# Attention half blocks: value products and normalizing before the next score products

## The chip, the cores and the metric

One Trainium2 chip; the kernel runs on one of its cores. The metric is the device time of the whole program in microseconds (us), the median of several runs.

## What is computed

The reference is windowed attention over four batches of 768 tokens with eight heads of 64, followed by a mixture of eight experts, of which each token takes two. Cut to what matters:

```python
scores = scale * np.matmul(q, k.transpose(0, 1, 3, 2))
keep = is_global | is_local          # 8 first keys, and 96 keys back from the query
scores = np.where(keep, scores + bias, -1e9)
a = np.exp(scores - np.max(scores, axis=-1, keepdims=True))
a = a / (np.sum(a, axis=-1, keepdims=True) + 1e-09)
x = np.matmul(a, v)                  # [4, 8, 768, 64] -> [3072, 512]
logits = x @ w_gate + np.log1p(np.exp(x @ w_noise)) * noise
# the two largest logits of a token choose its experts and weigh them
out[mask] += top2_w * (np.maximum(x[mask] @ w1[e], 0.0) @ w2[e])
```

## The kernel before

The tokens are taken in 24 blocks of 128 queries, six to a batch. A block's eight heads are taken in two halves of four heads, so attention is a loop over 48 **half blocks**, written `for n in range(0, NPAIR, 2)` with n = 0, 2, ... 94. The order of the instructions on each engine is the order in which the program emits them; nothing reorders them later. Attention lies in the first 150 us of the span, the experts behind it.

The work is software-pipelined. Half block n of the loop emits, in this order:

- **score(n + 2)**: VectorE adds the bias to the scores of the next half block and takes the maximum of each row (L862, four instructions on two PSUM banks, x = 0 and 1, with two query halves s each); ScalarE takes the exponentials (L865, four instructions). Behind each of the four a `tick` may emit one step of a routing program that is under way, mostly a small VectorE instruction.
- **trans(n), trans(n + 1)**: the **transposes** of the probabilities on TensorE (L878: six of 128x128, or four in the first block of a batch), each half into its own one of two PSUM banks, and ScalarE's two copies of them to SBUF (L880).
- **gate_t**, in every second half block: four **gate transposes** of a finished block (L380) and ScalarE's copy of them (L389, tile `pair`).
- **product(n + 4)**: the **score products** of queries by keys two half blocks ahead (L848, 16 records on 64x64 tiles of the array) into the two banks of the ring "sc", which score(n + 2) must have read.
- **norm(n - 4)**: VectorE's division by the row sums (L910, L912, L915), with three ticks.
- **attend(n - 2)**: the **value products** (L899). In the first block of a batch they are 16 records on tiles of 128 rows and 64 columns. In every other block they come in two parts of 16 records: the **short part** (64 or 40 rows by 64 columns) and the **tall part** (128 or 104 rows by 64 columns).
- **gate_s** with halves (L426, four short products on 128x64 tiles; seven half blocks) and **gate_l** (L410, the **gate products**, 16 records on 128x32 tiles that read the tile `pair`, and ScalarE's copy of them, L413; mostly every fourth half block). Steps of the routing that remain follow in `finish`.

In the last half block, n = 94, attend stands before norm. With 48 half blocks, 45 (n = 2 to 90) have both value products and score products; in eight of these the value products are of a batch's first block.

Of the kernel before, what the change touches and what calls it, by code (L numbers as in the profile page):

```python
# [35 lines left out]
def tile_local_global_attention_then_moe(  # L36
# [45 lines left out]
    def bank(tag):  # L82
        ring = rings[tag]
        key = tuple(ring)
        turns[key] = turns.get(key, -1) + 1
        return psum.tile([P, 512], F32, name=tag, tag=f"b{ring[turns[key] % len(ring)]}", bufs=1)
# [139 lines left out]
    def words(x):  # L226
        return x.bitcast(U16).rearrange("p (d h) -> p h d", h=2)

    def planes(x):
        return x.rearrange("p (h d) -> p h d", h=2)  # L230

    def halved(to, frm):

        for c in range(KC):
            c = slice(c * P, (c + 1) * P)
            nc.gpsimd.tensor_copy(to[:, :, c], frm[:, :, c])  # L236
# [131 lines left out]
    def partner(g):  # L368
        if not windowed or g in ALONE:
            return None  # L370
        a = [a for a, z in SEG if a <= g < z][0]
        return (g - a) % 2

    def gate_t(g):
        x = rowed[g] = XR.pop(g).rearrange("p h d -> p (h d)")
        stored[g] = gp.tile([P, 2 * Dm], U16, name="xt", bufs=4)
        halved(planes(stored[g]), words(x))
        ps = bank("m").rearrange("p (k t) -> p k t", k=KC)
        for k in range(KC):
            nc.tensor.transpose(ps[:, k], x[:, k * P:(k + 1) * P], ident)  # L380
        j = partner(g)
        if j is None:
            XT[g] = ys[2].rearrange("p (k t) -> p k t", k=KC)
            to = XT[g]
        else:
            if j == 0:
                XT[g + 1] = pairs[0].rearrange("p (k j t) -> p k j t", k=KC, j=2)
            to = XT[g + 1 - j][:, :, j]
        nc.scalar.activation(to, ps, AF.Copy)  # L389
# [263 lines left out]
    with ExitStack() as actx:  # L653
# [127 lines left out]
        def empty_rows():  # L781
            nc.gpsimd.memset(zero, 0.0)
            o = xd[:DUMP].rearrange("(p r) d -> p r d", p=P)
            nc.sync.dma_start(o, zero.bitcast(U16)[:, None, :].to_broadcast(o.shape))
# [30 lines left out]
        def tick(place):  # L815
            for y in sorted(active, key=lambda y: y[1] != CLOSE):
                if y[0].ready <= place:
                    return go(y)
# [8 lines left out]
        def geo(n):  # L827

            g, u = divmod(n, HP)
            b, i = divmod(g, NB)  # L830
            return g, u, b, i
# [52 lines left out]
        def attend(n):  # L884

            g, u, b, i = geo(n)
            ps = pav[g, u // 2] = bank("av")[:, :4 * D1].rearrange("p (h d) -> p h d", h=4)
            at = [AT.pop(n + x) for x in range(2)]
            heads = [(at[x], 2 * y + x, y * Q) for x in range(2) for y in range(2)]
            parts = [[(vs[g], 0, P, 0)], [(vs[g], 0, P, 1)]]  # L890
            if i:
                parts = [[(vs[g], 0, Q, 2), (vp[g], 0, NP + NG, 0)], [(vp[g], Q, NP + NG, 2), (vs[g], 0, P, 1)]]
            n = len(parts[0])
            for k in range(n):
                for a, h, q0 in heads:
                    c = slice((u // 2 * 4 + h) * D1, (u // 2 * 4 + h + 1) * D1)
                    for s in range(2):
                        t, r, z, part = parts[s][k]
                        nc.tensor.matmul(ps[s * Q:(s + 1) * Q, h], a[r:z, part * P + q0:part * P + q0 + Q], t[r:z, c],  # L899
                                         start=k == 0 and (n == 1 or h == 0), stop=k + 1 == n,  # L900
                                         tile_position=(r, s * Q), skip_group_check=True)

        def norm(n):

            g, u, b, i = geo(n)
            ps = pav.pop((g, u // 2))
            if u == 0:
                XR[g] = ys[g % 2].rearrange("p (h d) -> p h d", h=H)
            den = aw.tile([P, 4], F32, name="den", bufs=2)
            nc.vector.tensor_scalar(den, ps[:, :, D], 1e-9, None, op0=OP.add)  # L910
            tick(4)
            nc.vector.reciprocal(den, den)  # L912
            tick(5)
            h0 = 2 * u
            nc.vector.tensor_mul(XR[g][:, h0:h0 + 4], ps[:, :, :D],  # L915
                                 den[:, :, None].to_broadcast([P, 4, D]))
            tick(6)
# [3 lines left out]
        def at(n, f, *a):  # L921
            todo.setdefault(n, []).append((f, a))

        NPAIR = NT * HP
# [65 lines left out]
        if not windowed:  # L990
            gate_consts()
            route_consts()
            empty_rows()
            empty_first()
            for j in range(NZ):
                zero_out(j)
            for g in range(NT):
                whole(g)
            load_w(NU)
            for j in range(FC):  # L1000
                split(0, 1, j)
            load_w(NU)
            for t in range(TA):
                turn(0, t)
        else:
            for k in range(HP):
                at(k, biases, bias, dist, (2 * k, 2 * k + 1))
            at(4, gate_consts)
            at(10, route_consts)
            at(66, empty_rows)  # L1010
            at(80, empty_first)
            for g in range(NT):
                b, i = divmod(g, NB)
                n = g * HP
                if g + 3 < NT:
                    at(n + 2, load_v, g + 3)
                if i % NBH == 0 and g + NBH < NT:
                    for k in range(NBH):
                        at(n + 4 * k, load_qk, *divmod(g // NBH + 1, 2), k)
            for j in range(NZ):  # L1020
                at(70 + 4 * j, zero_out, j)
            for j, (n, x, y) in enumerate(((8, 16, 18), (14, 22, 24), (28, 40, 50), (36, 52, 64))):
                at(n, load_w)
                at(x, split, 0, 1, j, nc.gpsimd)
                at(y, split, 0, 1, j + NU, nc.gpsimd)
            ends = [z - 1 for a, z in SEG]

            product(0)  # L1030
            product(2, "av")
            score(0)
            for n in range(0, NPAIR, 2):
                g, odd = divmod(n // 2 - LAG, 2)
                begin()
                if n + 2 < NPAIR:
                    score(n + 2)
                trans(n)
                trans(n + 1)
                if g >= 0:  # L1040
                    if odd:
                        if g in ends:
                            gate_s(g)
                            active.append((Steps(route(ends.index(g))), ends.index(g)))
                    else:
                        gate_t(g)
                if n + 4 < NPAIR:
                    product(n + 4)
                if n == NPAIR - 2:
                    attend(n - 2)  # L1050
                if n >= 4:
                    norm(n - 4)
                if 2 <= n < NPAIR - 2:
                    attend(n - 2)
                if g >= 0 and odd and g not in ends:
                    gate_s(g, True)
                if g >= 0 and not odd:
                    gate_l(g, (lambda *x: at(n + 4, *x)) if n + 4 < NPAIR else None)
                if n < NPAIR - 2:
                    finish()  # L1060
                for x in n, n + 1:
                    for f, a in todo.pop(x, []):
                        f(*a)
            for x, _ in [y for y in active if y[1] <= CLOSE]:
                for _ in x:
                    pass
            active[:] = [y for y in active if y[1] > CLOSE]
            begin()
            norm(NPAIR - 4)
            for t in range(TA):  # L1070
                turn(0, t, bank("sc" if t > 1 else "at"))
                if t == 1:
                    gate_t(NT - 2)
            attend(NPAIR - 2)
            gate_l(NT - 2)
            begin()
            norm(NPAIR - 2)
            finish()
            finish()
            routes[NT - 1] = route(len(SEG) - 1)  # L1080
            assert len(routes) == 1 and not todo
            pending = [x for x, _ in active] + [Steps(x) for x in routes.values()]
# [447 lines left out]
    with tc.If(left > 0), tc.tile_pool(name="lc", bufs=1) as lc:  # L1530
# [18 lines left out]
        for e in range(E):  # L1549
            n = nc.values_load(more[0:1, e:e + 1], min_val=0, max_val=N)  # L1550
# [72 lines left out]
```

## Time and profile before

| | us |
|---|---|
| median of 3 runs | 698.28 (698.16 to 698.64) |
| the profiled execution | 696.72 |
| its span, first to last instruction | 695.0 |
| TensorE busy in the span | 682.1 (98%) |
| VectorE / ScalarE / GpSimd busy | 460.0 / 423.7 / 323.8 |
| mean granted TensorE clock | 0.996 of full speed |

PE is TensorE's matmul, PEld its weight load, DVE VectorE, ACT ScalarE, POOL GpSimd. L848 is line 848 of the kernel. Matmuls are pipelined, so the start of the next phase, and not the end of a record, tells how long a phase held TensorE.

### The profile page before, as it was taken

What the parts mean: (1) busy time and instruction counts of PE and PEld (TensorE: products, weight loads), DVE (VectorE), ACT (ScalarE), POOL (GpSimd) and SP (SyncE); (2) the same over time, 40 slices, a digit from 0 to 9 for tenths busy, and PEclk for the clock granted to TensorE, in tenths of its full rate; (3) what the DMA queues carried; (4) which work ended last, traced back from release to release, by engine and by line L of the source; (5) the groups of instructions that cost most, each with busy time, mean ns of one, the idle gap of its engine ahead of it and who ended that gap; (6) DMA issues with size and microseconds to landing.
All of it is one profiled execution on the core that took longest, in us unless ns stands there. A gap on an engine that the chain in (4) does not pass through costs nothing. (4 is left out here: it accounts for less than half of the span.)

```text
span 695.0 us, 16022 instructions
## 1 busy us (share of the span) xinstructions
PE 682.1 (98%) x5701; PEld 615.7 (89%) x5701; DVE 460.0 (66%) x1412; ACT 423.7 (61%) x912; POOL 323.8 (47%) x408
## 2 busy tenths in 40 slices
PE   7999999999999999999999999999999999999995
PEld 5888888888889999999999998999998899889984
DVE  6668788968938578557846693777367757847600
ACT  6888787762346576557754764586458557745510
POOL 3352737350188672264536445552745344541222
PEclk9999999999999999999999999999999999999998
DMA  9999988859393986347845974596559557843233
GB/s 255 320 293 314 277 250 271 304 182 331 130 292 72 178 186 151 63 111 182 174 76 114 166 170 79 151 172 117 93 154 245 88 106 181 171 74 91 32 47 49
DMA packets 132889, 116.61 MB, mean 168 GB/s; under 512 B 51866, under 2 KB 97050, under 8 KB 132800
## 3 DMA queue, kind: packets, MB, share of 16 engines
q1 hardware_dynamic: 121392, 89.35, 46.8%
q0 software_dynamic: 11264, 25.89, 20.9%
q8 instruction: 47, 0.77, 0.5%
q14 instruction: 42, 0.34, 0.2%
q10 hardware_dynamic: 144, 0.26, 0.2%
HBM read 71.07 MB, written 33.10 MB: 150 GB/s over the span
## 5 line engine op out<-in xcount | busy, mean ns | idle before, releaser
L1426 PE MATMUL bank<-xh,wall 128*128 128x384 f32 (+4 forms) x784 | 216.0, 342 | 0.0
L1426 PEld LDWEIGHTS bank<-xh,wall 128*128 128x128 f32 x784 | 144.1, 188 | 3.2
L1426 PE MATMUL bank<-xl,wall 128*128 128x384 f32 (+4 forms) x392 | 133.4, 340 | 0.0
L1145 POOL DMA_INDIRECT out_dram<-y,ids x40 | 65.1, 1626 | 123.1 <-ACT y L1142 120.2
L1169 PE MATMUL av<-w2h,hh 128*128 128x512 f32 x304 | 119.6, 393 | 0.0
L1169 PE MATMUL av<-w2h,hl 128*128 128x512 f32 x304 | 119.1, 392 | 0.0
L1169 PE MATMUL av<-w2l,hh 128*128 128x512 f32 x304 | 119.0, 392 | 0.0
L197 DVE TENSOR_TENSOR wall<-raw,wall 128x512 fp32r<-128x512 f32 (+1 forms) x84 | 75.9, 910 | 52.4 <-ACT wall L196 51.9
L196 ACT ACTIVATE wall<-raw 128x512 fp32r<-128x512 f32 (+1 forms) x84 | 57.9, 699 | 45.7 <-POOL raw L1279 45.7
L1117 DVE SCALAR_TENSOR_TENSOR hl<-bank,hh 128x384 fp32r<-128x384 f32 (+4 forms) x84 | 47.1, 561 | 51.0 <-ACT hh L1113 50.5
L865 ACT ACTIVATE a<-ns,mx 128x168 f32<-128x168 f32 (+1 forms) x192 | 67.8, 421 | 14.5 <-DVE mx L862 14.1
L1426 PEld LDWEIGHTS bank<-xl,wall 128*128 128x128 f32 x392 | 73.9, 188 | 2.9
L251 POOL DMA_INDIRECT xg<-xd,ids x49 | 52.9, 1079 | 41.7 <-DVE place L302 29.8
L1169 PEld LDWEIGHTS av<-w2h,hl 128*128 128x128 f32 x304 | 57.1, 188 | 12.6
L862 DVE CUSTOM_DVE_ANT_0 ns<-sc,bias 128x168 f32<-128x168 f32 (+1 forms) x188 | 51.8, 320 | 24.6 <-PE sc L848 10.0
L1169 PEld LDWEIGHTS av<-w2l,hh 128*128 128x128 f32 x304 | 57.1, 188 | 9.3 <-DVE w2l L197 0.3
L1169 PEld LDWEIGHTS av<-w2h,hh 128*128 128x128 f32 x304 | 57.1, 188 | 9.2
L1113 ACT ACTIVATE hh<-bank 128x384 fp32r<-128x384 f32 (+4 forms) x84 | 41.8, 498 | 37.1 <-DVE bank L1500 24.2
L1278 POOL TENSOR_TENSOR raw<-raw 128x256 f32<-128x256 f32 x28 | 22.4, 802 | 83.0 <-DVE wall L197 82.4
L899 PE MATMUL av<-vs,at 128*64 128x65 f32 (+1 forms) x768 | 57.1, 224 | 0.2 <-issue 0.2
L236 POOL COPY xt<-y 128x256 uint16<-128x256 uint16 x96 | 35.0, 401 | 46.8 <-DVE y L915 45.4
L899 PEld LDWEIGHTS av<-vs,at 128*64 128x64 f32 (+1 forms) x768 | 50.8, 136 | 2.8 <-issue 1.9
(219 smaller groups left out, 1463.4 us busy)
## 6 DMA issues: line engine op xcount, KB each, us to landing
raw<-in_w SPq DMA_DIRECT2D x64, 256.0 KB
raw<-in_w SPq DMA_DIRECT2D x32, 512.0 KB
out_dram<-zero SPq DMA_DIRECT2D x14, 512.0 KB
vs<-in_v SPq DMA_DIRECT2D x24, 260.0 KB
xd<-xt SPq DMA_DIRECT2D x24, 256.0 KB
qbuf<-in_q SPq DMA_DIRECT2D x23, 256.0 KB
ks<-in_k SPq DMA_DIRECT2D x20, 272.0 KB
xe<-y SPq DMA_DIRECT2D x17, 256.0 KB
```

The costliest lines, as they stand in the source:

```text
L196: nc.scalar.activation(hi, src, AF.Copy)
L197: eng.tensor_sub(lo, src, hi.bitcast(F32))
L236: nc.gpsimd.tensor_copy(to[:, :, c], frm[:, :, c])
L251: nc.gpsimd.indirect_dma_start(out=xg[e, t].bitcast(U16)[:m], out_offset=None, in_=xd[:n], in_offset=bass.IndirectOffsetOnAxis(ap=r, axis= ...
L862: nc.vector.tensor_tensor_reduce(out=ns[x][:, s, :w], in0=ps[:, s], in1=bias[:, u + x, s] if i else bias0[:, u + x, s], scale=-scale, scal ...
L865: nc.scalar.activation(A[n + x][:, s * w:(s + 1) * w], ns[x][:, s, :w], AF.Exp, bias=mx[x][:, s:s + 1], scale=-1.0)
L899: nc.tensor.matmul(ps[s * Q:(s + 1) * Q, h], a[r:z, part * P + q0:part * P + q0 + Q], t[r:z, c], start=k == 0 and (n == 1 or h == 0), stop ...
L1113: nc.scalar.activation(inner(e)[0][j][:, f, :src.shape[1]], src, AF.Relu)
L1117: nc.vector.scalar_tensor_tensor(lo, src, 0.0, hi.bitcast(F32), op0=OP.max, op1=OP.subtract)
L1145: ins = nc.gpsimd.indirect_dma_start(out=out, out_offset=bass.IndirectOffsetOnAxis(ap=r, axis=0), in_=y, in_offset=None, bounds_check=N + ...
L1169: nc.tensor.matmul(ps, x[j][:, f, cols], w[:, f], start=n == 0, stop=n == 3 * FC - 1)
L1426: nc.tensor.matmul(ps, wb[c % 2][u][:, 2 * a + k], x[v][:, 2 * b + k], start=start and n == 0, stop=stop and n == 5, skip_group_check=True)
```

## The change

In every half block norm(n - 4) and attend(n - 2) are emitted before product(n + 4). The special place of attend in the last half block goes away: it now follows norm there as well. Nothing is added or left out.

```diff
+                if n >= 4:
+                    norm(n - 4)
+                if n >= 2:
+                    attend(n - 2)
                 if n + 4 < NPAIR:
                     product(n + 4)
-                if n == NPAIR - 2:
-                    attend(n - 2)
-                if n >= 4:
-                    norm(n - 4)
-                if 2 <= n < NPAIR - 2:
-                    attend(n - 2)
```

## Rows read from the trace of the kernel before

**Rows 1.** The page: busy time of each engine.

```profile
PE 682.1 (98%) x5701; PEld 615.7 (89%) x5701; DVE 460.0 (66%) x1412; ACT 423.7 (61%) x912; POOL 323.8 (47%) x408
```

**Rows 2.** Busy time by stretches behind attention: length, engines, PE clock, DMA.

```profile
160.00:200.00 40.00, 39.72 (x195) 32.11 (x195) 30.19 (x117) 12.28 (x25) 11.23 (x19) 1.00 0.76 267
200.00:600.00 400.00, 400.00 (x2229) 373.46 (x2228) 268.11 (x461) 250.23 (x472) 208.70 (x193) 1.00 0.68 142
```

**Rows 3.** TensorE in order of time (start, length, operation), an inner block.

```profile
104.43 0.87 PE L878 MATMUL at<-ident,a 128*128 128x128 f32 x6
105.23 0.80 PE L848 MATMUL sc<-ks,qbuf 64*64 64x168 f32 x16
105.86 0.22 PE L899 MATMUL av<-vs,at 64*64 64x65 f32 x1
...
106.44 0.27 PE L899 MATMUL av<-vs,at 128*64 128x65 f32 x1
...
106.90 0.22 PE L899 MATMUL av<-vs,at 128*64 128x65 f32 x1
107.05 0.87 PE L878 MATMUL at<-ident,a 128*128 128x128 f32 x6
107.76 0.60 PE L380 MATMUL m<-ident,y 128*128 128x128 f32 x4
108.29 0.67 PE L848 MATMUL sc<-ks,qbuf 64*64 64x128 f32 x16
```

**Rows 4.** The same view, value products of a batch's first block.

```profile
44.77 0.80 PE L848 MATMUL sc<-ks,qbuf 64*64 64x168 f32 x16
45.51 0.69 PE L899 MATMUL av<-vs,at 128*64 128x65 f32 x16
46.12 0.88 PE L878 MATMUL at<-ident,a 128*128 128x128 f32 x6
```

**Rows 5.** The same view, a half block without score products.

```profile
148.18 0.27 PE L899 MATMUL av<-vs,at 64*64 64x65 f32 x1
...
148.79 0.27 PE L899 MATMUL av<-vs,at 128*64 128x65 f32 x1
```

**Rows 6.** The same view, short gate products behind the tall part.

```profile
29.37 0.22 PE L899 MATMUL av<-vs,at 128*64 128x65 f32 x1
29.42 0.26 PE L426 MATMUL lg<-sel,aside 128*64 128x32 f32 x4
```

**Rows 7.** The same view, two half blocks where score products stop midway.

```profile
15.34 1.11 PE L848 MATMUL sc<-ks,qbuf 64*64 64x168 f32 x13
...
16.99 0.27 PE L899 MATMUL av<-vs,at 128*64 128x65 f32 x1
...
134.15 0.85 PE L848 MATMUL sc<-ks,qbuf 64*64 64x168 f32 x13
...
135.54 0.27 PE L899 MATMUL av<-vs,at 128*64 128x65 f32 x1
```

**Rows 8.** VectorE, ScalarE and TensorE in order of time, 45.7 to 48.9 us.

```profile
45.74 0.33 DVE L862 CUSTOM_DVE_ANT_0 ns<-sc,bias 128x168 f32<-128x168 f32 x1 [0.49 <-PE sc L848]
...
47.43 0.84 ACT L880 ACTIVATE at<-at 128x384 f32<-128x384 f32 x2
48.17 0.59 ACT L389 ACTIVATE pair<-m 128x512 f32<-128x512 f32 x1
...
48.81 0.64 PE L410 MATMUL m<-pair,wgn 128*32 128x128 f32 x16
```

**Rows 9.** Busy time between starts of two scores; ScalarE's gate copy behind.

```profile
54.34:57.46 3.12, 3.12 (x73) 2.75 (x70) 3.08 (x26) 2.66 (x7) 0.64 (x2) 1.00 1.07 378
...
60.33 0.60 ACT L389 ACTIVATE pair<-m 128x512 f32<-128x512 f32 x1
...
122.49:125.98 3.49, 3.49 (x71) 2.94 (x68) 3.49 (x35) 2.28 (x6) 0.74 (x2) 1.00 1.06 373
...
128.55 0.59 ACT L389 ACTIVATE pair<-m 128x512 f32<-128x512 f32 x1
```

## The prediction

> **What bounds the kernel now.** I read the page's busy times first: TensorE is busy 98% of the span [rows 1]. Then the busy times by stretch: in the experts it has 0.28 us without work between 160 and 600 us [rows 2], so nothing there takes up a delay of attention; what TensorE loses in the loop, the end loses. A busy TensorE says nothing about its pace, so I read its instructions in order of time, as starts of phases. An inner half block without gate work is: transposes 104.43, score products 105.23, short value part 105.86, tall part 106.44, next transposes 107.05; that is 0.80 + 0.63 + 0.58 + 0.61 = 2.62 us [rows 3]. No phase waits for another engine there. The loop is a stream of back-to-back TensorE work, and its time is the sum of phases plus what the joints between them cost.
>
> **The joints.** Inside the tall part records step by about 0.05 us per pair, and the short gate products, on the same 128x64 tiles, follow the last one after 29.42 - 29.37 = 0.05 us [rows 6]. The transposes, on 128x128 tiles, follow after 107.05 - 106.90 = 0.15 us [rows 3]: a change of tile shape costs 0.10 here. Score products followed by the short part, both 64 rows high, hold TensorE for 0.63 us; followed by value products of full height, 45.51 - 44.77 = 0.74 us [rows 3, 4]: 0.11 more. Before the change a half block pays at three joints (transposes to scores, short to tall part, tall part to transposes), and scores to short part is free. After it there are four: transposes to short part, short to tall, tall to scores, scores to transposes.
>
> The Trainium skill, "TensorEngine Tiling (Array Packing)", section Tiling Modes, says that changing the tiling mode, and not just the tile, drains TensorE, which speaks against this order. The rows agree at 0.10 to 0.11 us per change; the page gives no figure, and without its rule the fourth joint would add nothing to the sum.
>
> **New half block, inner.** Transposes 0.80 (they lead into 64-row tiles as before). Short part behind transposes: 148.79 - 148.18 = 0.61 [rows 5]. Tall part 0.61, if leaving it for score products costs what leaving it for transposes does. Score products 0.74 in front of full-height tiles [rows 4]. Sum 2.76, against 2.62: **+0.14**. Where short gate products follow (seven half blocks), the tall part used to leave for free and the score products now do not: +0.14 + 0.10 = **+0.24**. In a batch's first block the same joints are paid in both orders (0.74 + 0.61 becomes 0.61 + 0.74): **0**, eight times. So 30 x 0.14 + 7 x 0.24 = **+5.9 us**. The joint of tall part to score products is in no row: with no change cost at all (0.05, rows 6) the sum is 45 x 0.10 less, +1.4; with the dearest step of the rows, 0.20 from transposes to score products (they take 0.80 where the next transposes take 0.71, so 0.09 over an ordinary step), it is 45 x 0.05 more, +8.2. I take the middle, since the same instructions are leaving the array.
>
> **Waits that go.** In eight half blocks the score products stop midway for VectorE, which is behind with routing steps and has not read the second bank. The two phases from score products to tall part then take 16.99 - 15.34 = 1.65 us in the worst and 135.54 - 134.15 = 1.39 in the mildest, against 1.21 [rows 3, 7]; the eight sum to 2.5, and the first half blocks have one more of 0.4. Put 1.2 us later in the half block, the score products find the bank read. **-2.9 us**; if none went, 0.
>
> **Waits that come.** VectorE's score starts 45.74 - 44.77 = 0.97 us after the score products start [rows 4, 8]. These now stand directly before the transposes, 0.74 ahead of them, so score starts 0.22 after the transposes of its half block; before, it could start 0.97 - 1.82 = 0.85 ahead of them. ScalarE runs in order: exponentials, two copies of the transposes, the gate copy. All move back by 1.07 us. Who waits for them?
>
> - The gate products need the gate copy. From score to the end of that copy: 48.17 + 0.59 - 45.74 = 3.02 us, and TensorE follows 0.05 later [rows 8]. New: 0.22 + 3.07 = 3.29 after the transposes begin. TensorE gets there at 0.71 + 0.53 (transposes and gate transposes, rows 3) + 0.61 + 0.61 + 0.74 = 3.20. A wait of 0.1 in a light half block, some 0.3 where routing steps stand between VectorE's four instructions: 8 x 0.2 = 1.6.
> - In three half blocks VectorE comes late as well. From one score to the next it worked 3.12 us on end (3.08 busy, rows 9); the new half block before is 2.76, so score starts 0.36 late, and from score to the gate copy's end there are 60.33 + 0.60 - 57.46 = 3.47. The gate products can start at 0.22 + 0.36 + 3.47 + 0.05 = 4.10 instead of 3.20: 0.9. The same pattern returns once at 94 us, and the third has 3.49 of work, 0.73 late, and 128.55 + 0.59 - 125.98 = 3.16: 4.16, so about 1.0 [rows 9]. Together 2.8.
> - The next transposes need their bank copied, and all score work of the half block before. The first copy ends about 47.43 + 0.42 - 45.74 = 2.1 after score starts [rows 8], so at 2.3 of a 2.76 us half block: no wait. Only the short half blocks of a batch's start, without gate work, are quicker (0.58 + 0.61 + 0.74 = 1.93); three of them, 0.4 in all as far as VectorE and ScalarE have not caught up.
>
> **+4.8 us**; below it 0, if score starts earlier than I take it; above it see the second rival.
>
> **Costed at nothing.** norm emits VectorE work alone, whose order against score does not change; its ticks can emit routing matmuls, but in this trace these come behind the value products. No DMA is emitted by what moves, so the SP and POOL queues keep their order. The value products start 0.6 earlier; the copies they need ended in the half block before. In the last half block norm comes first, and its bank is another one.
>
> **Sum:** 5.9 - 2.9 + 4.8 = **+7.8 us** on the profiled 696.72, so 704.5. The median of the runs lies 1.56 above that execution: 698.28 + 7.8 = **706.1**.
>
> **Rivals.**
> - *The gate and transposes never wait* (score is quicker off the mark): 5.9 - 2.9 = +3.0, 701.3. For it: VectorE gets 0.14 us more per half block in which to catch up. Against: the gate copy's chain is 3.02 us even where nothing delays it.
> - *The score chain becomes the loop's bound*: plain half blocks too wait for copied banks. The slack is 2.76 - 2.3 = 0.4; extra ScalarE work eats it in some. At 0.1 us in each of 45: +4.5 more, 710.6.
> - *Faster*: leaving the tall part for scores and scores for transposes costs nothing in the new places (0.52 and 0.63). An inner half block is then 0.80 + 0.61 + 0.52 + 0.63 = 2.56, 0.06 less than now; 30 of these, 7 at about +0.03 and eight first blocks at -0.20 give -3.2; with the waits, -3.2 - 2.9 + 4.8 = -1.3, 697.0, and 692.2 if no new wait comes. It decides once the joints cost less than they do now by 0.04 per half block. Against it stand the 0.74 and the 0.15 in the rows.
> - *The delay is absorbed later*: 698.3. Against it stands a TensorE with 0.28 us to spare in 440.
>
> **Chances.** Forecast 0.64, with its own range 704 to 708.5; no new waits 0.15; chain-bound 0.12; faster 0.04; absorbed 0.05. 0.2% is 1.4 us, about what a measurement of this kernel can tell from none. Slower 0.64 + 0.15 + 0.12 = 0.91, same 0.05, faster 0.04. The range takes in the first rival and ends below the second: 701.0 to 709.6.
>
> **What would show it.** Right: score products followed by transposes 0.74 later; the tall part followed by score products 0.15 after its last pair; no score products that stop midway; gate products that wait for the gate copy, some 0.1 to 0.3 and three near 1 us; VectorE idle before score until the score products end. The start of the experts' first products moves by the whole sum. Wrong: a tall-to-score joint of 0.05, or transposes that wait in plain half blocks.

## The result, and the profile after

The changed kernel takes 706.68 us (median of 4 runs, 706.16 to 707.02) against 698.22 for the kernel before on the same chip (4 runs): a ratio of 1.0119, with an interval of 1.0103 to 1.0135. It is 8.46 us slower. The forecast was 706.1, in a range of 701.0 to 709.6.

The first two rows are the page's busy time of each engine and the group of VectorE's score (busy, mean ns of one, then the idle time of VectorE ahead of it and what ended it).

```profile
PE 686.7 (97%) x5701; PEld 611.4 (87%) x5701; DVE 459.7 (65%) x1412; ACT 424.4 (60%) x912; POOL 323.4 (46%) x408
...
L862 DVE CUSTOM_DVE_ANT_0 ns<-sc,bias 128x168 f32<-128x168 f32 (+1 forms) x188 | 51.9, 321 | 38.0 <-PE sc L848 29.0
```

Instruction counts are those of [rows 1], so nothing was added. TensorE is still busy nearly throughout. VectorE's idle time in front of score, ended by the score products, is now 29.0 us; on the page of before that entry is 10.0. TensorE's own order of time shows what an inner half block has become:

```profile
33.16 0.87 PE L878 MATMUL at<-ident,a 128*128 128x128 f32 x6
33.96 0.27 PE L899 MATMUL av<-vs,at 64*64 64x65 f32 x1
...
34.58 0.27 PE L899 MATMUL av<-vs,at 128*64 128x65 f32 x1
...
35.04 0.22 PE L899 MATMUL av<-vs,at 128*64 128x65 f32 x1
35.19 0.80 PE L848 MATMUL sc<-ks,qbuf 64*64 64x168 f32 x16
35.92 0.87 PE L878 MATMUL at<-ident,a 128*128 128x128 f32 x6
```

The starts give 0.80 + 0.62 + 0.61 + 0.73 = 2.76 us, where [rows 3] gave 2.62. The tall part is followed by the score products 0.15 after its last pair; this is the joint that no row of before showed. VectorE's next score starts at 36.15 (the first row of the next view), 0.23 behind the transposes.

```profile
36.15 0.33 DVE L862 CUSTOM_DVE_ANT_0 ns<-sc,bias 128x168 f32<-128x168 f32 x1 [0.85 <-PE sc L848]
```

Next, TensorE's waits up to 160 us, by line: total, times, longest. They count time without work only, after the modelled end of the last matmul.

```profile
...
PE m L410 <- ACT pair L389: 4.1, 8, 0.8
PE lg L423 <- ACT aside L413: 0.7, 1, 0.7
PE lg L628 <- ACT aside L472: 0.3, 1, 0.3
PE at L878 <- ACT at L880: 0.2, 1, 0.2
```

None of these four rows is in the same view of before; the row ahead of them, a load at the start, stands in both. The gate products wait for the gate copy, as forecast. The second row, short products that wait for ScalarE's copy of the gate products, and the third, a step of the routing, were not foreseen. One heavy half block, VectorE, ScalarE and TensorE in order of time:

```profile
61.07 0.31 DVE L862 CUSTOM_DVE_ANT_0 ns<-sc,bias 128x168 f32<-128x168 f32 x1
...
63.94 0.60 ACT L389 ACTIVATE pair<-m 128x512 f32<-128x512 f32 x1
...
60.58 0.88 PE L878 MATMUL at<-ident,a 128*128 128x128 f32 x6
...
63.05 0.80 PE L848 MATMUL sc<-ks,qbuf 64*64 64x168 f32 x16
64.59 0.65 PE L410 MATMUL m<-pair,wgn 128*32 128x128 f32 x16 [0.74 <-ACT pair L389]
```

From score to the end of the gate copy there are 63.94 + 0.60 - 61.07 = 3.47 us, the same as in the half block of [rows 9]. The gate products start 0.05 after it, 4.01 behind the transposes (forecast 4.10). The step from score products to gate products is 64.59 - 63.05 = 1.54; without a wait it is 0.73, so the wait is 0.81.

The two half blocks of [rows 7], where score products had stopped midway, in the changed kernel:

```profile
16.36 0.80 PE L848 MATMUL sc<-ks,qbuf 64*64 64x168 f32 x16
...
143.46 0.80 PE L848 MATMUL sc<-ks,qbuf 64*64 64x168 f32 x16
```

All 16 records run without a break. The delay then stays: the first products of the experts start at

```profile
164.99 0.50 PE L1130 MATMUL at<-wall,xh 128*128 128x512 f32 x1
```

in the changed kernel, and in the kernel before at

```profile
155.57 0.50 PE L1132 MATMUL at<-wall,xh 128*128 128x512 f32 x1
```

That is 9.4 us later, and the span grows from 695.0 to 705.2. The two profiled executions lie a little further apart than the medians (707.02 - 696.72 = 10.3 against 8.46).

### The profile page after: what moved, and what is told of

Its sections match the earlier page's. It is cut to its first block, busy times and chain, and to the rows that moved or that the text cites. A ratio compares the mean times of both kernels' runs of the same rounds, so it can differ in the third digit from the quotient of the medians.

```text
span 705.2 us, 16044 instructions
## 1 busy us (share of the span) xinstructions
PE 686.7 (97%) x5701; PEld 611.4 (87%) x5701; DVE 459.7 (65%) x1412; ACT 424.4 (60%) x912; POOL 323.4 (46%) x408
## 4 chain that ended last, share of the span: by engine, by line
PE 75%; issue 6%; DVE 5%; ACT 5%; DMA 3%; POOL 2%; SPq 1%; POOLq 0%; ACTq 0%; DVEq 0%
PE bank L1424 28%; PE av L1167 22%; PE av L1190 7%; PE av L899 5%; PE at L878 4%; PE sc L848 3%; ACT a L865 2%; SPq L356 1%; ACT at L880 1%; POOL out_dram L1143 1%; PE m L410 1%; DMA out_dram<-zero 1%; PE m L380 1%; DVE ns L862 1%; DMA xt<-xg 1%
## 5 line engine op out<-in xcount | busy, mean ns | idle before, releaser
L899 PEld LDWEIGHTS av<-vs,at 128*64 128x64 f32 (+1 forms) x768 | 47.5, 136 | 7.6 <-issue 4.7
```

## The experiments

Two theories stood against each other after the result. By the *joint theory* the loss is a fourth change of tile shape in the half block plus gate products that wait; by the *lateness theory* the whole loss comes from score products that stand 1.2 us later, with VectorE and ScalarE late behind them. The first three kernels below and the first try with later gate products ran on one chip, where the kernel before took 697.54 us (16 runs); the other three ran on another, where it took 696.66 (23 runs). Each is compared with the kernel before on its own chip.

**Normalizing alone in front.**

```diff
+                if n >= 4:
+                    norm(n - 4)
                 if n + 4 < NPAIR:
                     product(n + 4)
-                if n == NPAIR - 2:
-                    attend(n - 2)
-                if n >= 4:
-                    norm(n - 4)
-                if 2 <= n < NPAIR - 2:
+                if n >= 2:
                     attend(n - 2)
```

> The order of before, with norm alone moved in front of the score products. Joint theory and lateness theory alike: norm emits VectorE work alone and its place against score does not change, so the time is that of before, 698.2 within 1 us. If the normalizing steps or their ticks carried part of the loss, some us more.

Measured: 698.01 us (11 runs), ratio 1.0002 (0.9992 to 1.0011). The place of norm is worth nothing that can be measured, 0.8 us at most; the loss belongs to the order of score products and value products.

**The joints without the lateness.** The order of before, with the tall part in front of the short one. Score products stay early, but each half block outside a batch's first block has four changes of tile shape.

```diff
-                parts = [[(vs[g], 0, Q, 2), (vp[g], 0, NP + NG, 0)], [(vp[g], Q, NP + NG, 2), (vs[g], 0, P, 1)]]
+                parts = [[(vp[g], 0, NP + NG, 0), (vs[g], 0, Q, 2)], [(vs[g], 0, P, 1), (vp[g], Q, NP + NG, 2)]]
```

> The order of before, score products early, but the tall part of the value products in front of the short one. Joint theory: score products to tall part and short part to transposes both change the tile shape, four changes for three, 0.14 us in each of 37 half blocks and about 0.15 more where short gate products follow: 698.2 + 6.2 = 704.4, with no wait of the gate products for the gate copy. Lateness theory (the loss comes from score starting later): score starts as early as before, so 698.2.

Measured: 702.46 us (5 runs), ratio 1.0070 (1.0057 to 1.0084), 4.9 us over before. TensorE in an inner half block:

```profile
33.37 0.87 PE L878 MATMUL at<-ident,a 128*128 128x128 f32 x6
34.18 0.80 PE L848 MATMUL sc<-ks,qbuf 64*64 64x168 f32 x16
34.91 0.27 PE L899 MATMUL av<-vp,at 104*64 104x65 f32 x1
...
35.53 0.27 PE L899 MATMUL av<-vp,at 40*64 40x65 f32 x1
...
35.99 0.22 PE L899 MATMUL av<-vp,at 40*64 40x65 f32 x1
36.14 0.87 PE L878 MATMUL at<-ident,a 128*128 128x128 f32 x6
```

The half block is 2.77 us long, as in the changed kernel (2.76), though nothing is late: score products into full-height tiles take 0.73, and leaving the 64-row part for the transposes takes 0.15. Gate products do not wait in this trace. So a fourth joint costs its 0.14 us with early score products too, and the lateness theory, which expected no loss, falls. The loss stayed 1.3 us under the expectation. The trace shows the joints in full, 0.145 us in each of 30 half blocks and 0.295 in seven, 6.4 together. What the expectation left out is that the score products stop less in the longer half blocks: six of the eight stops get shorter or go, 1.1 us in all. Short gate products that wait in one of the last half blocks take 0.7 back, so not all of the 1.3 is accounted for.

**Score products half as late, with three joints.** Tall part first, then the score products, then the short part (the parts are swapped as in the kernel above, and attend becomes a generator that stops between them).

```diff
+                if k:
+                    yield
...
+                parts_of = attend(n - 2) if n >= 2 else iter(())
+                next(parts_of, None)
+                if n + 4 < NPAIR:
+                    product(n + 4)
+                for _ in parts_of:
+                    pass
```

> norm, then the tall part of the value products, the score products, the short part. Score products are 0.6 us later than before instead of 1.2, but scores to short part is free again, three changes of shape as before. Joint theory: an inner half block takes 0.80 + 0.62 + 0.62 + 0.58 = 2.62, as before; short gate products cost 0.15 more seven times (+1.0), three heavy half blocks still wait some 0.75 for the gate copy (+2.3), the stops of the score products go (-2.9): 698.2 + 0.4, between 697 and 700. Lateness theory: half of the lateness, half of the loss, 702.5.

Measured: 699.80 us (6 runs), ratio 1.0037 (1.0024 to 1.0049), 2.26 over before. Over its own before, the joint theory expected 0.4 (between -1.2 and 1.8) and the lateness theory 4.3, so the time lies between the two and does not decide. The trace does: plain half blocks take 2.62 us as before, though their score products are 0.6 later, and what is longer is mainly the seven with short gate products, by 0.15 each, and four with gate products that wait, by 0.4 to 0.6. In TensorE's order of time the first two rows, 33.20 and 33.82, show the free joint again: 64-row score products followed by the 64-row short part, after 0.62 us. (The order tall part, short part, score products would have three joints too, with score products as late as in the changed kernel. It was not run.)

```profile
33.20 0.80 PE L848 MATMUL sc<-ks,qbuf 64*64 64x168 f32 x16
33.82 0.22 PE L901 MATMUL av<-vs,at 64*64 64x65 f32 x1
...
34.40 0.88 PE L878 MATMUL at<-ident,a 128*128 128x128 f32 x6
```

**The same, with the short gate products directly behind the tall part.** They run on 128x64 tiles, as the tall part does, so they should be free there.

```diff
+                next(parts_of, None)
                 if g >= 0 and odd and g not in ends:
                     gate_s(g, True)
+                if n + 4 < NPAIR:
+                    product(n + 4)
```

> As e3_split, with the short gate products directly behind the tall part, whose tile shape they share. Joint theory: a change of shape less and a free start in seven half blocks, 0.15 us each: 1.0 us less than e3, 1.3 us above the kernel before. Without a cost of joints: as e3, 2.3 us above before.

Measured: 697.14 us (11 runs), ratio 1.0008 (0.9999 to 1.0017): 0.5 over before, where the last kernel was 2.26 over its own and the expectation was 1.3. In the trace each of the seven half blocks is back at its length of before, 1.05 us together, as expected; another 0.8 went in the last half blocks of attention, and its cause is open. A plain half block runs like this:

```profile
33.09 0.80 PE L848 MATMUL sc<-ks,qbuf 64*64 64x168 f32 x16
33.71 0.22 PE L901 MATMUL av<-vs,at 64*64 64x65 f32 x1
...
34.14 0.22 PE L901 MATMUL av<-vp,at 40*64 40x65 f32 x1
34.29 0.55 PE L878 MATMUL at<-ident,a 128*128 128x128 f32 x3
```

From the transposes before it, at 31.67 (next fence), to these are 34.29 - 31.67 = 2.62 us, to the hundredth the half block of [rows 3], though its score products stand behind the tall part of the value products.

```profile
31.67 0.88 PE L878 MATMUL at<-ident,a 128*128 128x128 f32 x6
32.47 0.27 PE L901 MATMUL av<-vp,at 104*64 104x65 f32 x1
```

**The waits alone: gate products later.** The changed kernel, with the gate products of seven blocks one half block later. It was tried twice. At first gate_l moved whole, and with it the stores of the block that it issues:

```diff
+                for x in held_l:
+                    gate_l(x, (lambda *x: at(n + 4, *x)) if n + 4 < NPAIR else None)
+                held_l.clear()
                 if n + 4 < NPAIR:
                     product(n + 4)
...
-                    gate_l(g, (lambda *x: at(n + 4, *x)) if n + 4 < NPAIR else None)
+                    if partner(g) == 1 and g not in ends:
+                        held_l.append(g)
+                    else:
+                        gate_l(g, (lambda *x: at(n + 4, *x)) if n + 4 < NPAIR else None)
```

> The changed kernel with seven of the eleven gate products (those of blocks that end no segment) emitted one half block later, between value products and score products, so that the gate copy is long done. Their waits were 0.11, 0.24, 0.81, 0.40, 0.81, 0.40 and 0.87 us, 3.6 in all; one more change of shape each costs about 0.1 us. Theory that these waits cost what the trace shows: 706.7 - 3.6 + 0.8 = 703.9. Rival (the delay sits in VectorE's and ScalarE's chain and only shows there): transposes or short gate products wait instead, 706 to 707.

Measured: 709.17 us (5 runs), ratio 1.0161 (1.0147 to 1.0175), worse than the change itself. The expectation failed, and not for the gate products: transposes that start at 113.71 us in the changed kernel start at 111.59 here, 2.1 us sooner, as the waits of gate products before it had gone. Then VectorE's last step of norm stood still for 4.46 us, for a store of the buffer that it writes. The rows are VectorE's, and SyncE's issue of the store that it waited for, half a block late:

```profile
123.99 0.42 DVE L915 TENSOR_TENSOR y<-av,den 128x256 f32<-128x256 f32 x1 [4.46 <-DMA xe<-y]
...
116.86 0.38 SPq L396 DMA_DIRECT2D xe<-y  x1
```

In the changed kernel the same store is issued at 117.30, VectorE writes the buffer at 121.96, 4.66 later, and is never idle ahead of this line. Here it wanted the buffer at 119.53, 2.67 after the issue.

```profile
117.30 0.35 SPq L396 DMA_DIRECT2D xe<-y  x1
```

By its semaphore the store had landed at 121.23 in the changed kernel, 3.9 us after its issue, and at 123.87 here, 7.0 after. With 3.9 the wait would have been 1.2 us (an estimate from these times); the rest of the 4.46 is the slower landing, and why it was slower was not tried.

So the second try leaves the stores where they were and moves the products alone:

```diff
+        if products:
+            gate_p(g)
+
+    def gate_p(g):
...
+                for x in held_l:
+                    gate_p(x)
+                held_l.clear()
```

> As e4_gate_late, but only the gate products move to the next half block; the two stores of the block stay where they were (in e4 the store of the block moved too, VectorE's next division into that buffer waited 4.5 us for it, and TensorE fell to half its clock behind that). The first six waits disappeared in e4 one for one (2.7 us up to 124 us), with no extra change of shape. Theory that the waits cost what the trace shows: 706.7 - 3.6 = 703.1. Rival (they come back elsewhere): 706 to 707.

Measured: 701.50 us (6 runs), ratio 1.0072 (1.0059 to 1.0085), 4.8 over its before, as expected; the change itself is 8.46 over its own. The 3.6 us between are what the seven waits sum to in the changed kernel, 0.11 + 0.24 + 0.81 + 0.40 + 0.81 + 0.40 + 0.87 = 3.6. That it comes out so evenly is in part luck: in the trace the first six go one for one, 2.8 us, half of the seventh comes back as longer half blocks behind it, and 1.4 us of waits that were not moved went too, in the last half blocks of attention. The heavy half block of above, with products that follow on the tall part without a wait:

```profile
64.84 0.22 PE L903 MATMUL av<-vs,at 128*64 128x65 f32 x1
64.99 0.65 PE L414 MATMUL m<-pair,wgn 128*32 128x128 f32 x16
65.57 0.66 PE L852 MATMUL sc<-ks,qbuf 64*64 64x168 f32 x12
```

The two tries differ in the place of the stores only, so the moved stores cost 11.6 - 4.8 = 6.8 us.

**Both costs taken away.** The split order, the short gate products behind the tall part, the seven gate products a half block later and their short products also a half block later, so two behind the old place of the gate products. Score products still stand behind the tall part.

```diff
+                next(parts_of, None)
+                for x in held_s:
+                    gate_s(x, True)
+                held_s[:] = held_l
+                for x in held_l:
+                    gate_p(x)
+                held_l.clear()
+                if n + 4 < NPAIR:
+                    product(n + 4)
+                for _ in parts_of:
+                    pass
```

> As e6_split_gs, with the seven gate products one half block and their short gate products two half blocks later, so that neither waits for ScalarE (the three heavy half blocks of e3 waited 0.5 us each). Joint and wait theories: 1.5 us less than e6, 0.2 us below the kernel before, no measurable difference from it. If the waits come back elsewhere: as e6.

Measured: 696.47 us (12 runs), ratio 0.9999 (0.9988 to 1.0010). The loss is gone; a gain is not measurable. As the score products are half as late here as in the changed kernel, this does not show that its whole order can be had for nothing.

## Why the prediction was right

It was right in sign and size, and its two causes were shown singly: the fourth joint by a kernel that adds it with nothing late and by two that are half as late without it, the waits of the gate products by a kernel that moves these out of the way. By its own steps:

- **Joints, +5.9 forecast, 6.4 measured.** Leaving the tall part for score products takes 0.150 in all 45 half blocks; 0.15 had been taken, between bounds of 0.05 and 0.20. An inner half block without gate work is 0.145 longer (0.14 forecast). The seven with short gate products are 0.30 longer instead of 0.24, as these now follow a change of shape themselves. So 30 x 0.145 + 7 x 0.30 = 6.4.
- **Waits that go, -2.9 forecast, -4.0 measured.** All eight stops are gone, and the one at the start. Another 1.1 us went that was not forecast; 0.63 of it is one slow stretch of value products at 145 to 147 us of before, and its cause stays open.
- **Waits that come, +4.8 forecast, 7.1 measured.** In the eight light half blocks the gate products wait 2.5 us together, with single waits between 0 and 0.62, not 0.2 each; the three heavy ones 0.81, 0.81 and 0.87, 2.5 together, where 2.8 was forecast; transposes 0.4, as forecast. Not forecast: 0.35 for a routing step, 0.5 for score products that stop in two other half blocks, and 0.8 for the short gate products of the second row of waits.
- **Sum.** 6.4 - 4.0 + 7.1 = 9.5 in the loop, where the transposes of the last half block start 9.4 later; the forecast was 7.8. The medians, 8.46 apart, lie between. The terms of waits were both too small, by 1.1 and 2.3 us, and as they have opposite signs, half of the larger miss was made good by the smaller. So it is partly luck that the forecast of 706.1 met 706.68 within 0.6 us: in the trace it was 1.6 short. The step that was mis-sized most is the wait of a light half block: it had been worked out from a chain without routing steps and 0.3 where some stand between, and came to 0.31 on average (2.5 / 8), with single ones twice that. A wait of the short gate products, 0.8 in one half block, was in no term at all.

Of the rivals, "the gate never waits" falls with 5.0 us of such waits; "the chain becomes the bound" with plain half blocks of 2.76 us and no wait; "faster" with the joints; "absorbed" with 9.4 us that the experts did not give back. The late short gate products (0.8 here, and 1.1 us of idle time in the kernel with the tall part first) follow a copy that ScalarE started late; what held this copy was not tried.

For the joints, the Trainium skill, "TensorEngine Tiling (Array Packing)", section Tiling Modes, has the rule that a change of mode drains TensorE. The runs agree as far as a change costs time: a half block with four takes 2.76 and 2.77 us, in two orders of the work, and one with three 2.62, in two others.

## What to carry to other kernels

When TensorE runs short matmuls of several tile shapes in a row, count the changes of shape in an order before its dependencies: phases that share a shape belong next to each other, and one change more cost 0.14 of the 2.62 us of a half block here, over 5%, and the list of waits shows nothing of it. When a product is moved back, follow the chain behind it to its last reader on the same engine, and move that reader as well. When a function is moved, look at the transfers that it issues: a store that had been free cost 6.8 us half a block later.

## What the runs showed of the hardware

The chip granted TensorE less clock in the first try with later gate products. The view is of busy time by stretch: length, busy time of PE, PEld, DVE, ACT and POOL, granted clock, DMA.

```profile
118.00:122.00 4.00, 4.00 (x74) 3.34 (x72) 1.40 (x11) 2.30 (x7) 4.00 (x9) 1.00 1.02 332
122.00:125.00 3.00, 1.58 (x30) 1.25 (x22) 1.01 (x3) 0.28 (x1) 1.22 (x3) 1.00 1.04 372
125.00:128.00 3.00, 1.40 (x19) 1.00 (x18) 2.75 (x13) 1.65 (x6) 0.76 (x3) 0.86 1.07 367
128.00:131.00 3.00, 3.00 (x22) 2.54 (x16) 2.25 (x16) 2.25 (x9) 0.90 (x3) 0.50 1.07 384
131.00:133.00 2.00, 2.00 (x21) 1.67 (x20) 1.15 (x6) 1.37 (x3) 0.54 (x2) 0.50 0.51 186
133.00:137.00 4.00, 4.00 (x76) 3.09 (x74) 2.57 (x21) 2.19 (x6) 0.12 (x1) 0.88 0.62 202
```

In the second and third of these stretches TensorE worked 1.58 and 1.40 us of 3.00. Then its granted clock fell to 0.50, which is the lower level of 1.2 GHz, and it stayed there while TensorE was busy again; six transposes took 1.48 us there instead of 0.87. From the transposes at 122.13 to those at 134.30 two half blocks took 12.2 us, where the changed kernel takes 5.8 (124.64 to 130.44): 6.4 us more, behind 3.0 us without work. That the two waits brought the fall of the clock about is read from one trace and was not tried by itself.

A change of shape also showed in the records behind it: four short gate products took 0.085 us from first to last start after a change, and 0.037 behind tiles of their own shape.
